# Tying a transform's input differences and conversions into program order, and loading the second stage's input one step earlier

## The chip, the cores and the metric

The kernel runs as one program on one core of a Trainium2 chip. The metric is the device time of one execution in microseconds (us), as a median over runs. Engines are written as in the profile: PE (TensorE matmul), PEld (its weight load), DVE (VectorE), ACT (ScalarE), POOL (GpSimd), SP (SyncE, which only issues DMAs here).

## The reference, cut to what matters

Three models stand one behind the other, over 8 sequences ("batches" below) of 3072 tokens with 256 channels, all in float32.

```python
X = np.fft.rfft(x, axis=1)                       # the transform, per batch and channel
y = np.fft.irfft(X * (filt_r + 1j * filt_i), n=3072, axis=1)
x_prev = shifted y, zeros in front
xk = mu_k * y + (1 - mu_k) * x_prev;  xr = mu_r * y + (1 - mu_r) * x_prev
k = np.maximum(xk @ w_k, 0);  v = (k * k) @ w_v  # 256 -> 1024 -> 256
r = 1 / (1 + np.exp(-(xr @ w_r)))
z = r * v
h = maximum of z @ w1, z @ w2, z @ w3            # 256 -> 768
out = h @ w_out                                  # 768 -> 256
```

## The kernel before, in words

**Float32 by parts.** Most matrix products take each operand as a high part and a low part (`mm3`, three matmuls for one product). `split` (L249) makes the parts of a source: ACT copies it to the high part with a cast, and POOL (or DVE) subtracts the high part from the source for the low one.

**The transform.** The first batch has its own code (`fft_first`). Batches 2 to 8 use `fft`, in three phases. In the a-phase 12 units are formed: `a_diff` (8 of 12) subtracts two halves of a loaded tile `xz` into `xd` with one DVE instruction; `a_sum` (4 of 12) adds three slices of two tiles `xr` into `xs` with four DVE instructions; `a_halves` splits the result into `xah` (ACT) and `xal` (POOL); `a_mm` multiplies it one step later (three matmuls, `pa<-xah`, `pa<-xal`, `pa<-xah`), and ACT copies the product out (`ao`) and stores it to DRAM (`s1a`, `s1b`). In the b-phase (12 steps) `b_load` loads the stored tile `xb` and splits it into `xbh` and `xbl`, `b_mm` multiplies it and applies the filter; in the c-phase `c_mm` multiplies the split result `yh`, `yl`.

**The main work.** Each batch is cut into 4 chunks, 32 in all. For a chunk `kv` runs the first feed-forward model: products `pk`, `kr` (ACT and DVE), its parts `khi` and `klo`, then `pv` three blocks later; `x2` multiplies by the gate (`gate<-pv`). For each pair of chunks `second` runs the maxima as seven products per block (`pb`, `pa`, `pe` over streamed weights `ws`, evacuated to `m`, `sc`, `u`, `v`), then `po`. Weights arrive through SP: `piece_of` asks for them 8 tiles ahead into 10 buffers (L337).

**What sets the order.** `drive` writes the transform of the next batch in small weighted pieces between the pieces of the main work. That is the program order. A scheduler of the framework then orders each engine's queue anew by a timeline that it computes, with program order as priority: an instruction whose inputs it holds to be ready may be placed ahead of work written in front of it. `tc.keep_in_program_order(ins)` takes this freedom from one instruction: it stays behind the instruction written last on its engine. Once ordered, an engine runs its queue in that order, and an instruction that waits holds all behind it. Buffers come from rotating pools (`fin`, which holds `xd`, `xs` and `xb`, has 2; `fhi`, `flo` and `filt` have 3).

Of the kernel before, what the change touches and what calls it, by code (L numbers as in the profile page):

```python
# [9 lines left out]
F32 = mybir.dt.float32  # L10
# [4 lines left out]
ALU = mybir.AluOpType  # L15
# [8 lines left out]
NK = 2 * N2  # L24
NR = 3
NS = N1 // NR * 2
GA = NG // NR
# [170 lines left out]
def tile_spectral_moe(ctx: ExitStack, tc, x, xr, xz, filt, ones, wa, wa1, wi, wbc, wb1, wc1, filt1, filt0, mu, w_k, w_v, w_r, w1, w2, w3, w_out, out):  # L198
    nc = tc.nc
    B = xr.shape[0]  # L200
    P = 128
    C = 256
# [13 lines left out]
    fp = ctx.enter_context(tc.tile_pool(name="fp", bufs=2))  # L216
# [10 lines left out]
    def mm3(o, parts, rhs_parts, onto=False, more=False):  # L227


        n = len(parts)  # L230
        for k in range(n):
            (wh, wl), (xh, xl) = parts[k], rhs_parts[k]
            mm(o, wh, xh, k == 0 and not onto, False, more)
            mm(o, wh, xl, False, False, more)
            mm(o, wl, xh, False, k == n - 1, more)
# [10 lines left out]
        nc.scalar.dma_start(mu_s, mu)  # L246
        nc.vector.tensor_scalar(nmu_s, mu_s, -1.0, 1.0, op0=ALU.mult, op1=ALU.add)

    def split(hi, lo, src, lo_eng=None):  # L249
        nc.scalar.copy(hi, src)  # L250
        (lo_eng or nc.gpsimd).tensor_tensor(lo, src, hi.bitcast(F32), ALU.subtract)  # L251


# [146 lines left out]
    def fft(b):  # L400

        s1a = dp.tile([NM, 4, GA, C], F32, tag="s1a", name=f"s1a_{b}")
        s1b = dp.tile([NM, 4, GB, C], F32, tag="s1b", name=f"s1b_{b}")
        s2 = dp.tile([NM, 4, NG, C], F32, tag="s2", name=f"s2_{b}")
        s2_of[b] = s2
        st = {}
        pieces = []
        H = NK // 2

        def x_load(t):  # L410
            st["x", t] = fp.tile([NK, NR, C], F32, tag="filt", name="xr", bufs=3)
            nc.sync.dma_start(st["x", t], xr[b, t])

        def z_load(t):
            st["z", t] = fp.tile([NK, 2, 2, C], F32, tag="filt", name="xz", bufs=3)
            nc.sync.dma_start(st["z", t], xz[b, t])

        def a_halves(u, v):
            hi = fp.tile([NK, 2, C], F32R, tag="fhi", name="xah", bufs=3)
            lo = fp.tile([NK, 2, C], F32R, tag="flo", name="xal", bufs=3)  # L420
            split(hi, lo, v, nc.gpsimd)
            st["a", u] = hi, lo

        def a_diff(u, t):
            z = st.pop(("z", t))
            v = fp.tile([NK, 2, C], F32, tag="fin", name="xd")
            nc.vector.tensor_tensor(v, z[:, 0], z[:, 1], ALU.subtract)  # L427
            a_halves(u, v)

        def a_sum(u, t):  # L430
            v = fp.tile([NK, 2, C], F32, tag="fin", name="xs")
            for k in range(2):
                x0 = st.pop(("x", t + k))
                nc.vector.tensor_tensor(v[:, k], x0[:, 0], x0[:, 1], ALU.add)
                nc.vector.tensor_tensor(v[:, k], v[:, k], x0[:, 2], ALU.add)
            a_halves(u, v)

        def a_mm(u):
            t, k = divmod(u, 3)
            w = 0 if k == 1 else 1  # L440
            hi, lo = st.pop(("a", u))
            p = ps.tile([NK, 2, C], F32, tag="pm", name="pa")
            mm3(p, [(wa_s[:, 0, w], wa_s[:, 1, w])], [(hi, lo)])
            o = fp.tile([NK, 2, C], F32, tag="fo", name="ao")
            nc.scalar.copy(o, p)
            if w == 0:
                d = s1a[8 * t : 8 * t + 8].rearrange("(k j) r g c -> (j r g) k c", k=2)
            else:
                m = 8 * t + 2 * k
                d = s1b[m : m + 4].rearrange("(k j) r g c -> (j r g) k c", k=2)  # L450
            nc.scalar.dma_start(d, o)

        NU3 = NM // 8 * 3
        NBS = NG // 2
        for u in range(NU3 + 1):
            def pa(u=u):
                t, k = divmod(u, 3)
                if u == 0:
                    z_load(0)
                if u < NU3:  # L460
                    if k == 0:
                        x_load(2 * t)
                        x_load(2 * t + 1)
                        a_diff(u, 2 * t)
                    elif k == 1:
                        z_load(2 * t + 1)
                        a_sum(u, 2 * t)
                    else:
                        if 2 * t + 2 < NM // 4:
                            z_load(2 * t + 2)  # L470
                        a_diff(u, 2 * t + 1)
                if u >= 1:
                    a_mm(u - 1)
            pieces.append((0.69, pa))

        def b_load(s):
            w = fp.tile([NK, 4, 2, NK], F32R, tag="wbc", name="wbc", bufs=3)
            nc.sync.dma_start(w.bitcast(F32), wbc_d[s].bitcast(F32))
            f = fp.tile([NK, 2, 2, C], F32, tag="filt", name="filt", bufs=3)
            nc.sync.dma_start(f, filt[:, s])  # L480
            t = fp.tile([NK, 2, C], F32, tag="fin", name="xb")
            sv, k = (s1a, 2 * s) if 2 * s < GA else (s1b, 2 * s - GA)
            nc.sync.dma_start(t, sv.rearrange("m r g c -> (m r) g c")[:, k : k + 2, :])
            hi = fp.tile([NK, 2, C], F32R, tag="fhi", name="xbh", bufs=3)
            lo = fp.tile([NK, 2, C], F32R, tag="flo", name="xbl", bufs=3)
            split(hi, lo, t)
            st["b", s] = w, f, hi, lo

        def b_mm(s):
            w, f, hi, lo = st.pop(("b", s))  # L490
            p = ps.tile([NK, 2, C], F32, tag="pm", name="pb")
            for g in range(2):
                mm3(p[:, g], [(w[:, 0, g], w[:, 1, g])], [(hi[:, g], lo[:, g])], g > 0, True)

            fr, fi = f[:, 0], f[:, 1]
            H = NK // 2
            nc.vector.scalar_tensor_tensor(fi[:H], p[H:], -1.0, fi[:H], ALU.mult, ALU.mult)
            nc.vector.tensor_tensor(fi[H:], p[:H], fi[H:], ALU.mult)
            nc.vector.tensor_tensor(fr, p, fr, ALU.mult)
            (nc.gpsimd).tensor_tensor(fr, fr, fi, ALU.add)  # L500
            yh = fp.tile([NK, 2, C], F32R, tag="fhi", name="yh", bufs=3)
            yl = fp.tile([NK, 2, C], F32R, tag="flo", name="yl", bufs=3)
            split(yh, yl, fr)
            st["c", s] = w, yh, yl

        def c_mm(s):
            w, yh, yl = st.pop(("c", s))
            p = ps.tile([NK, 2, C], F32, tag="pm", name="pc")
            for g in range(2):
                mm3(p[:, g], [(w[:, 2, g], w[:, 3, g])], [(yh[:, g], yl[:, g])], g > 0, True)  # L510
            o = fp.tile([NK, 2, C], F32, tag="fo", name="co")
            nc.scalar.copy(o, p)
            nc.scalar.dma_start(s2.rearrange("m r g c -> (m r) g c")[:, 2 * s : 2 * s + 2, :], o)

        for s in range(NBS + 2):
            def pb(s=s):
                if s < NBS:
                    b_load(s)
                if 1 <= s <= NBS:
                    b_mm(s - 1)  # L520
            def pc(s=s):
                if s >= 2:
                    c_mm(s - 2)
            pieces.append((0.65, pb))
            if s == 0:

                pieces.append((6.0, lambda: None))
            pieces.append((0.65, pc))
        return pieces
# [456 lines left out]
    s, left = second(0)  # L986
    units += s
    units.append((0.0, lambda: combos(1)))
    for p in range(1, NPAIR):
# [5 lines left out]
        s, left = second(p)  # L995
# [21 lines left out]
    for b in range(B):  # L1017
        part = units[starts[b] : ends[b]]
        if b + 1 < B:
            side = fft(b + 1)  # L1020
            cut = cuts[b] + n2 - starts[b]
            if b == 0:
                for _, fn in part[:lead]:
                    fn()
                part, cut = part[lead:], cut - lead
            drive(part[:cut], side, sum(w for w, _ in part[:cut]), sum(w for w, _ in side))
            for _, fn in part[cut:]:
                fn()
        else:
            for _, fn in part:  # L1030
                fn()
# [50 lines left out]
```

## Time and profile before

| | |
|---|---|
| median of 3 runs | 3163.63 us (3161.4 to 3163.87) |
| the profiled execution | 3161.27 us, of which the span of instructions is 3159.5 us |
| PE busy / PEld busy | 3080.0 us (97%) / 3020.4 us (96%) |
| DVE / ACT / POOL busy | 1922.4 / 1884.8 / 1858.6 us (61%, 60%, 59%) |
| granted TensorE clock, mean | 0.99 of full speed |

Busy time is summed over instructions. A wait is put down to the engine or transfer that ended last before the waiting instruction began. In timelines a bracket behind a row is the idle time of the engine just before it and what ended it. Rows of a timeline that follow each other with the same shape are merged, with their count.

### The profile page before, as it was taken

The page shows a single profiled execution, that of the slowest core. Times are in us where ns is not written, and L with a number is a line of the kernel's source. Part 1 is how long each engine was busy: PE and PEld are TensorE (multiplying, and loading weights), DVE is VectorE, ACT ScalarE, POOL GpSimd, SP SyncE. Part 2 cuts the span into 40 slices and gives each one's busy share as a digit, 9 for nine tenths or more (in the row PEclk, how much of TensorE's full clock was granted, in tenths as well). Part 3 has the DMA queues.
Part 4 walks back from the last instruction along what each step waited for, and adds up shares of the span by engine and source line. Part 5 has one row for each costly group of instructions (what it writes and reads, how often), then busy time and mean ns, then how long its engine had stood idle before and what let it go on. Part 6 is the DMA issues. An engine that isn't in the chain of part 4 may idle for free.

```text
span 3159.5 us, 55818 instructions
## 1 busy us (share of the span) xinstructions
PE 3080.0 (97%) x19172; PEld 3020.4 (96%) x19172; DVE 1922.4 (61%) x3050; ACT 1884.8 (60%) x3968; POOL 1858.6 (59%) x1591
## 2 busy tenths in 40 slices
PE   6799999999999999999999999999999999999998
PEld 4699999999999999999999999999999999999998
DVE  4976676556664666556655566656666566555554
ACT  5556656566565566656666556566666566555554
POOL 3545765567554676556756566556765468444443
PEclk8899999999999999999999999999999999999999
DMA  9878787667776677758767587765887567555554
GB/s 298 267 260 285 235 305 227 188 197 251 260 233 184 224 240 227 254 171 259 251 221 220 183 263 261 227 205 183 262 268 237 180 214 232 178 169 165 161 170 122
DMA packets 400951, 705.92 MB, mean 223 GB/s; under 512 B 41472, under 2 KB 153120, under 8 KB 400032
## 3 DMA queue, kind: packets, MB, share of 16 engines
q1 hardware_dynamic: 333648, 621.26, 62.1%
q10 hardware_dynamic: 64576, 72.45, 6.5%
q0 software_dynamic: 2448, 8.65, 0.8%
q8 instruction: 155, 2.54, 0.3%
q14 instruction: 124, 1.02, 0.1%
HBM read 616.35 MB, written 92.14 MB: 224 GB/s over the span
## 4 chain that ended last, share of the span: by engine, by line
PE 81%; DVE 6%; DMA 5%; POOL 3%; issue 3%; ACT 1%; ACTq 0%; SPq 0%; POOLq 0%; DVEq 0%
PE pb L225 17%; PE pk L225 15%; PE pv L225 14%; PE po L225 12%; PE pe L225 8%; PE pa L225 5%; PE pr L225 4%; PE py L225 3%; DMA ws<-wud 3%; PE pc L225 2%; DVE sc L773 1%; POOL klo L251 1%; DMA s<-e 1%; DVE xd L427 1%; POOL hh L251 1%
## 5 line engine op out<-in xcount | busy, mean ns | idle before, releaser
L225 PE MATMUL pb<-x,ws 128*128 128x384 f32 x3456 | 751.7, 337 | 10.2 <-DMA ws<-wud 7.0
L251 POOL TENSOR_TENSOR hh<-m,hh 128x384 fp32r<-128x384 f32 x384 | 409.5, 1075 | 563.5 <-ACT hh L250 481.4
L251 POOL TENSOR_TENSOR klo<-kr,khi 128x384 fp32r<-128x384 f32 x492 | 520.8, 1064 | 233.2 <-ACT khi L250 205.1
L225 PEld LDWEIGHTS pb<-x,ws 128*128 128x128 f32 x3456 | 596.1, 188 | 20.5 <-issue 6.4
L741 DVE SCALAR_TENSOR_TENSOR kr<-pk,kr 128x384 f32<-128x384 f32 x512 | 281.4, 553 | 429.7 <-ACT kr L740 427.5
L225 PE MATMUL pv<-khi,ws 128*128 128x384 f32 x2048 | 481.3, 338 | 4.9 <-ACT khi L250 4.9
L225 PE MATMUL po<-wo_hi,hh 128*128 128x256 f32 x2304 | 481.4, 282 | 3.3 <-ACT hh L250 2.6
L250 ACT CAST khi<-kr 128x384 fp32r<-128x384 f32 x512 | 261.9, 513 | 226.8 <-DVE kr L741 191.9
L225 PEld LDWEIGHTS po<-wo_hi,hh 128*128 128x128 f32 x2304 | 391.1, 189 | 5.0 <-ACT hh L250 3.4
L225 PE MATMUL pe<-x,ws 128*128 128x384 f32 x1728 | 387.8, 338 | 3.5 <-DVE m L848 1.4
L225 PEld LDWEIGHTS pv<-khi,ws 128*128 128x128 f32 x2048 | 358.9, 188 | 8.5 <-ACT khi L250 6.4
L225 PE MATMUL pk<-xh,wk_hi 128*128 128x384 f32 x1024 | 341.2, 336 | 3.8 <-ACT xh L250 3.8
L225 PE MATMUL pk<-xl,wk_hi 128*128 128x384 f32 x1024 | 343.7, 336 | 0.9 <-DVE xl L251 0.9
L225 PE MATMUL pk<-xh,wk_lo 128*128 128x384 f32 x1024 | 343.3, 335 | 0.0
L225 PE MATMUL po<-wo_lo,hh 128*128 128x256 f32 x1152 | 316.8, 282 | 0.0
L740 ACT ACTIVATE kr<-pk 128x384 f32<-128x384 f32 x512 | 249.8, 489 | 108.8 <-POOL klo L251 56.8
L225 PEld LDWEIGHTS pe<-x,ws 128*128 128x128 f32 x1728 | 297.4, 188 | 8.8 <-DVE sc L855 3.1
L225 PE MATMUL pv<-klo,ws 128*128 128x384 f32 x1024 | 298.6, 338 | 2.4 <-DVE klo L251 1.3
L856 DVE TENSOR_TENSOR m<-sc,m 128x384 f32<-128x384 f32 x384 | 293.9, 768 | 8.4
L251 POOL TENSOR_TENSOR xl<-xm,xh 128x768 fp32r<-128x768 f32 x126 | 234.9, 1880 | 70.3 <-ACT xh L250 70.2
L250 ACT CAST hh<-m 128x384 fp32r<-128x384 f32 x384 | 192.6, 514 | 123.5 <-DVE m L856 85.6
L809 ACT COPY v<-pb 128x384 f32<-128x384 f32 x288 | 138.3, 480 | 188.8 <-PE pb L225 181.4
(134 smaller groups left out, 6143.1 us busy)
## 6 DMA issues: line engine op xcount, KB each, us to landing
ws<-wud SPq DMA_DIRECT2D x864, 256.0 KB, 3.8
ws<-wvd SPq DMA_DIRECT2D x512, 256.0 KB, 3.7
wbc<-wbcd SPq DMA_DIRECT2D x84, 512.0 KB, 5.5
filt<-in_filt SPq DMA_DIRECT2D x84, 512.0 KB, 4.3
ws<-wud SPq DMA_DIRECT2D x288, 128.0 KB, 3.7
xz<-in_xz SPq DMA_DIRECT2D x56, 512.0 KB, 5.2
cin<-s SPq DMA_DIRECT2D x64, 384.0 KB, 4.1
out_dram<-osb ACTq DMA_DIRECT2D x192, 128.0 KB, 2.9
```

Source lines behind the costliest of these rows:

```text
L225: nc.tensor.matmul(o, lhsT=wgt, rhs=rhs, start=start, stop=stop, skip_group_check=more)
L250: nc.scalar.copy(hi, src)
L251: (lo_eng or nc.gpsimd).tensor_tensor(lo, src, hi.bitcast(F32), ALU.subtract)
L427: nc.vector.tensor_tensor(v, z[:, 0], z[:, 1], ALU.subtract)
L740: nc.scalar.activation(r, p, AF.Relu)
L741: nc.vector.scalar_tensor_tensor(r, p, 0.0, r, ALU.max, ALU.mult)
L773: eng.tensor_tensor(t, a, b, ALU.subtract)
L809: nc.scalar.copy(st[to], st[of])
L856: nc.vector.tensor_tensor(m, c, m, ALU.max)
```

## The change

The subtraction in `a_diff` and the first addition of each pair in `a_sum` (DVE) are tied into program order. The cast that makes `xbh` from the loaded `xb` (ACT) is tied too. `b_load` now only loads `xb`, and a new `b_split` one step later loads the weights and the filter and splits; `b_mm` and `c_mm` follow one step later each, in 15 steps in place of 14.

```diff
-    def split(hi, lo, src, lo_eng=None):
-        nc.scalar.copy(hi, src)
+    def split(hi, lo, src, lo_eng=None, tied=False):
+        ins = nc.scalar.copy(hi, src)
+        if tied:
+            tc.keep_in_program_order(ins)
         (lo_eng or nc.gpsimd).tensor_tensor(lo, src, hi.bitcast(F32), ALU.subtract)
...
-            nc.vector.tensor_tensor(v, z[:, 0], z[:, 1], ALU.subtract)
+            tc.keep_in_program_order(nc.vector.tensor_tensor(v, z[:, 0], z[:, 1], ALU.subtract))
             a_halves(u, v)
...
-                nc.vector.tensor_tensor(v[:, k], x0[:, 0], x0[:, 1], ALU.add)
+                tc.keep_in_program_order(nc.vector.tensor_tensor(v[:, k], x0[:, 0], x0[:, 1], ALU.add))
                 nc.vector.tensor_tensor(v[:, k], v[:, k], x0[:, 2], ALU.add)
...
         def b_load(s):
+            st["f", s] = fp.tile([NK, 2, C], F32, tag="fin", name="xb")
+            sv, k = (s1a, 2 * s) if 2 * s < GA else (s1b, 2 * s - GA)
+            nc.sync.dma_start(st["f", s], sv.rearrange("m r g c -> (m r) g c")[:, k : k + 2, :])
+
+        def b_split(s):
+            t = st.pop(("f", s))
             w = fp.tile([NK, 4, 2, NK], F32R, tag="wbc", name="wbc", bufs=3)
             nc.sync.dma_start(w.bitcast(F32), wbc_d[s].bitcast(F32))
             f = fp.tile([NK, 2, 2, C], F32, tag="filt", name="filt", bufs=3)
             nc.sync.dma_start(f, filt[:, s])
-            t = fp.tile([NK, 2, C], F32, tag="fin", name="xb")
-            sv, k = (s1a, 2 * s) if 2 * s < GA else (s1b, 2 * s - GA)
-            nc.sync.dma_start(t, sv.rearrange("m r g c -> (m r) g c")[:, k : k + 2, :])
             hi = fp.tile([NK, 2, C], F32R, tag="fhi", name="xbh", bufs=3)
             lo = fp.tile([NK, 2, C], F32R, tag="flo", name="xbl", bufs=3)
-            split(hi, lo, t)
+            split(hi, lo, t, tied=True)
             st["b", s] = w, f, hi, lo
...
-        for s in range(NBS + 2):
+        for s in range(NBS + 3):
             def pb(s=s):
                 if s < NBS:
                     b_load(s)
                 if 1 <= s <= NBS:
-                    b_mm(s - 1)
+                    b_split(s - 1)
+                if 2 <= s <= NBS + 1:
+                    b_mm(s - 2)
             def pc(s=s):
-                if s >= 2:
-                    c_mm(s - 2)
+                if s >= 3:
+                    c_mm(s - 3)
```

The queues are ordered anew as a whole. **Place 1**, DVE in the first batch's `kv`, where the transform of the second batch begins; before (`hs` belongs to the conversion of weights, `xm` to the next chunk's input):

```order
L427 TENSOR_TENSOR xd<-xz 128x512
L251 TENSOR_TENSOR klo<-kr,khi 128x384
L434 TENSOR_TENSOR xs<-xr 128x256 x2
L435 TENSOR_TENSOR xs<-xs,xr 128x256
L741 SCALAR_TENSOR_TENSOR kr<-pk,kr 128x384
L435 TENSOR_TENSOR xs<-xs,xr 128x256
L715 SCALAR_TENSOR_TENSOR xm<-yt,nmu_s,xm 128x384 x4
L741 SCALAR_TENSOR_TENSOR kr<-pk,kr 128x384
L251 TENSOR_TENSOR klo<-kr,khi 128x384
L427 TENSOR_TENSOR xd<-xz 128x512
L741 SCALAR_TENSOR_TENSOR kr<-pk,kr 128x384
```

and now, from the same first `xd` on:

```order
L429 TENSOR_TENSOR xd<-xz 128x512
L253 TENSOR_TENSOR klo<-kr,khi 128x384
L748 SCALAR_TENSOR_TENSOR kr<-pk,kr 128x384
L722 SCALAR_TENSOR_TENSOR xm<-yt,nmu_s,xm 128x384 x4
L748 SCALAR_TENSOR_TENSOR kr<-pk,kr 128x384 x2
L253 TENSOR_TENSOR klo<-kr,khi 128x384
L368 TENSOR_TENSOR hs<-ps,hs 128x4x128
```

The four additions and the second difference have left this place; they now stand some 40 instructions of the main work later, in `second` of the first pair.

**Place 2**, PE in a later batch (the fourth that `fft` serves), at the fourth unit of the a-phase; before (`pa_` and `pb_` with numbers are products of `second`; `pa<-xah` and `pa<-xal` are the transform's):

```order
L225 MATMUL pb_15294<-x_15037,ws 128x384 x3
L225 MATMUL pe_15390<-x_15040,ws 128x384 x3
L225 MATMUL pa<-xah,wa_s 128x512
L225 MATMUL pa<-xal,wa_s 128x512
L225 MATMUL pa<-xah,wa_s 128x512
L225 MATMUL pb_15382<-x_15029,ws 128x384 x3
L225 MATMUL pa_15383<-x_15032,ws 128x384 x3
```

and now, the same unit:

```order
L225 MATMUL pv<-klo,ws 128x384 x2
L225 MATMUL pb_15294<-x_15043,ws 128x384 x3
L225 MATMUL pe_15346<-x_15046,ws 128x384 x3
L225 MATMUL pb_15338<-x_15037,ws 128x384 x3
L225 MATMUL pe_15390<-x_15040,ws 128x384 x3
L225 MATMUL pb_15382<-x_15029,ws 128x384 x3
L225 MATMUL pa_15383<-x_15032,ws 128x384 x3
L225 MATMUL pb_15338<-x_15043,ws 128x384 x3
L225 MATMUL pa<-xah,wa_s 128x512
L225 MATMUL pb_15448<-x_15022,ws 128x384 x3
```

The unit stands at about the same point of the main work, and its three matmuls no longer stand together: the one on the low part comes nine matmuls behind the first.

**Place 3**, DVE for the same unit; before:

```order
L856 TENSOR_TENSOR m<-sc,m 128x384
L852 TENSOR_TENSOR m<-pb_14410,m 128x384
L855 TENSOR_TENSOR sc<-pe_14489,v 128x384
L427 TENSOR_TENSOR xd<-xz 128x512
L856 TENSOR_TENSOR m<-sc,m 128x384
```

and now:

```order
L855 TENSOR_TENSOR m<-pe_15346,v 128x384
L859 TENSOR_TENSOR m<-pa_15339,m 128x384
L769 TENSOR_TENSOR gate<-pv,gate 128x384 x2
L429 TENSOR_TENSOR xd<-xz 128x512
L855 TENSOR_TENSOR m<-pe_15346,u 128x384
L862 TENSOR_TENSOR sc<-pe_15390,v 128x384
L863 TENSOR_TENSOR m<-sc,m 128x384
```

The difference stood in the blocks of the pair before (products 14410 and 14489); now it stands behind the gate product of the chunk that has just ended, among blocks 15339 to 15390.

## Rows read from the trace of the kernel before

**Rows 1.** The page, part 1: busy us, share, instructions.
```profile
PE 3080.0 (97%) x19172; PEld 3020.4 (96%) x19172; DVE 1922.4 (61%) x3050; ACT 1884.8 (60%) x3968; POOL 1858.6 (59%) x1591
```
**Rows 2.** Busy us by engine in stretches of the span, columns in the first row.
```profile
core 0: us, PE busy (x) PEld busy (x) DVE busy (x) ACT busy (x) POOL busy (x), PEclk, DMA share, GB/s
160.00:200.00 40.00, 35.88 (x236) 34.34 (x235) 37.92 (x51) 22.63 (x47) 27.88 (x24) 0.99 0.76 248
240.00:300.00 60.00, 59.35 (x368) 57.56 (x369) 46.94 (x67) 40.10 (x85) 40.28 (x33) 1.00 0.88 295
480.00:2743.00 2263.00, 2251.41 (x14174) 2225.34 (x14174) 1381.68 (x2197) 1387.50 (x2937) 1402.75 (x1191) 1.00 0.70 225
2743.00:3050.00 307.00, 307.00 (x1916) 307.00 (x1916) 160.15 (x272) 176.15 (x382) 145.45 (x133) 1.00 0.54 163
```
**Rows 3.** Waits of PE from 480 to 2743 us: total us, times, longest.
```profile
PE pb L225 <- DMA ws<-wud: 6.5, 11, 1.2
PE pa L225 <- DMA ws<-wud: 1.7, 3, 0.7
```
**Rows 4.** Timeline of DVE at place 1: start, us, instruction.
```profile
185.19 3.69 DVE L434 TENSOR_TENSOR xs<-xr 128x256 f32<-128x256 f32 x2
188.81 0.41 DVE L435 TENSOR_TENSOR xs<-xs,xr 128x256 f32<-128x256 f32 x1
...
189.94 3.99 DVE L715 SCALAR_TENSOR_TENSOR xm<-yt,nmu_s,xm 128x384 f32<-128x384 f32 x4
193.86 0.55 DVE L741 SCALAR_TENSOR_TENSOR kr<-pk,kr 128x384 f32<-128x384 f32 x1
...
195.94 2.31 DVE L427 TENSOR_TENSOR xd<-xz 128x512 f32<-128x512 f32 x1
198.17 0.54 DVE L741 SCALAR_TENSOR_TENSOR kr<-pk,kr 128x384 f32<-128x384 f32 x1
```
**Rows 5.** Timeline of PE and ACT at the same place.
```profile
195.26 0.62 PE L225 MATMUL pv<-khi,ws 128*128 128x384 f32 x2 [1.34 <-ACT khi L250]
...
198.75 0.51 ACT L250 CAST khi<-kr 128x384 fp32r<-128x384 f32 x1 [1.78 <-DVE kr L741]
...
199.32 0.56 PE L225 MATMUL pv<-khi,ws 128*128 128x384 f32 x1 [1.83 <-ACT khi L250]
```
**Rows 6.** Busy us from 180 to 240 us, `xd` alone, then `xs` alone (DVE, ACT, POOL).
```profile
180.00:240.00 60.00, 4.72 (x4) 1.86 (x3) 4.20 (x3) 0.97 0.80 273
...
180.00:240.00 60.00, 5.87 (x8) 0.64 (x1) 1.29 (x1) 0.97 0.80 273
```
**Rows 7.** Instructions of the a-phase over the run: count, ns min/median/max, first and last start.
```profile
L427 DVE TENSOR_TENSOR xd<-xz x56: 675/1406/2308, 182.9 to 2434.9; 128x512 f32<-128x512 f32 x56
...
L250 ACT CAST xah<-xd x56: 610/623/634, 191.2 to 2445.4; 128x512 fp32r<-128x512 f32 x56
L251 POOL TENSOR_TENSOR xal<-xd,xah x56: 1263/1298/1746, 191.9 to 2446.2; 128x512 fp32r<-128x512 f32 x56
```
**Rows 8.** Timeline at places 2 and 3, ACT, DVE, then PE.
```profile
1256.17 0.62 ACT L250 CAST xah<-xd 128x512 fp32r<-128x512 f32 x1
...
1271.28 1.02 DVE L762 TENSOR_TENSOR gate<-pv,gate 128x384 f32<-128x384 f32 x2 [0.68 <-PE pv L225]
...
1274.38 0.39 PE L225 MATMUL pa<-xah,wa_s 128*128 128x512 f32 x1
...
1283.95 1.72 PE L225 MATMUL pb<-x,ws 128*128 128x384 f32 x9
```
**Rows 9.** A wait of PE near place 2, and SP's waits from 1250 to 1280 us.
```profile
1277.08 1.12 PE L225 MATMUL pb<-x,ws 128*128 128x384 f32 x5 [0.79 <-DMA ws<-wud]
...
SPq L416 <- DVE xd L427: 3.6, 1, 3.6
```
**Rows 10.** A DMA (KB, median us to landing), and ACT's waits for `xb` over the run.
```profile
xz<-in_xz SPq DMA_DIRECT2D x56, 512.0 KB, 5.2
...
ACT xbh L250 <- DMA xb<-s1a: 15.0, 12, 2.2
```

## The prediction, made before the changed kernel ran

> **What bounds the kernel now.** I read the page's busy times first. PE is busy for 97% of the span, and no other engine for more than 61% [rows 1]. So the time is PE's work plus the moments in which PE stands still, and an edit that takes no matmul away can only move those moments. The second view, busy time by stretches, says where they are [rows 2]. From 160 to 200 us PE idles for 40 - 35.88 = 4.1 us, and DVE is busy for 37.92 of these 40. From 240 to 300 us PE idles for 0.65 us. From 480 to 2743 us, in which six of the seven changed transforms run, PE idles for 2263 - 2251.41 = 11.6 us in all. From 2743 to 3050 us no transform runs, and PE doesn't idle at all. The reader is to see how little there is to win. The third view, PE's waits from 480 to 2743 us, says what the 11.6 us are: 8.2 us (6.5 + 1.7 us, 14 waits) are for streamed weights `ws` [rows 3], which the change doesn't touch directly.
>
> [...]
>
> **Part 1: the early differences leave the first batch (place 1).** On DVE the four additions of `a_sum` took 3.69 us (two of them, merged) and 0.41 us for a third, with another like it, some 4.5 us. They stood in front of `xm` and of the `kr` at 193.86 us [rows 4]. PE then waited 1.34 us for `khi`, which is made from that `kr`, and again 1.83 us at 199.32 us, where `khi` had waited 1.78 us for the `kr` at 198.17 us; just ahead of this one DVE had run `xd` for 2.31 us [rows 4, 5]. The order shows both groups gone from here. DVE could then start the first `kr` up to 4.5 us and the second up to 2.3 us sooner, more than either wait. I take both waits as gone: -3.2 us. Bounds: -4.1 us (all idle time of the stretch) and 0, if `kr` is late by its own product.
>
> **Part 2: they reappear in a shorter stretch of the first batch.** From 180 to 240 us `xd` and `xs` took 4.72 + 5.87 = 10.6 us of DVE [rows 6]. All but the first `xd` (about 1 us) move behind 240 us. The stretch from 240 to 300 us had 46.94 us of DVE work [rows 2]; with 9.6 us more it is 56.5 of 60, or 94%. What PE loses beside a DVE that full isn't shown there, so I bound it by the two nearest rows. At 78% it lost 0.65 us in 60 us. At 95% (160 to 200 us) it lost 4.1 us in 40, which is 6.2 us in 60. The cost lies between 0 and 5.5 us; I take the middle, +2.8 us, since the order still has matmuls of `second` to fill with there, while the earlier stretch had products that hung on DVE directly.
>
> **Part 3: in the six later batches the a-phase loses its lead.** Before, the cast of the fourth unit's `xah` ended at 1256.79 us and its product began at 1274.38 us, 17.6 us later [rows 8]. Now the tied difference stands behind the two `gate` products, which wait for the last `pv<-klo` (place 3), and PE reaches the unit after 21 matmuls from there (place 2). One takes between 307.00 / 1916 = 0.16 us, an average with narrower ones among them [rows 2], and 1.72 / 9 = 0.19 us, which counts the drain of the last [rows 8]; I take 0.17 us, so 21 take 3.6 us. The chain against it is `gate` twice, 1.02 us [rows 8], `xd` 1.41 us and `xah` 0.62 us [rows 7], and three handovers of about 0.05 us (DVE's `kr` ends at 198.71 us, ACT's `khi` begins at 198.75 us [rows 4, 5]): 3.2 us. The unit comes 0.4 us early. Its low part takes POOL 1.30 us more [rows 7], 4.5 us, and is wanted nine matmuls later, at 5.2 us: early by 0.7 us. So a lead of 17 us becomes one of half a microsecond, at one of the tightest of 12 units. With `xd` at its longest, 2.31 us [rows 7], the unit is 0.5 us late. In a batch 8 of 12 units go through `xd`. If all 8 were 0.5 us late, six batches would lose 24 us; if none, nothing. I take one such delay for each batch, 0.5 us, hence +3 us, nearer to nothing: main chains with as many links through DVE, ACT and POOL cost PE next to nothing from 480 to 2743 us, where waits for `ws` alone make 8.2 of 11.6 us [rows 2, 3].
>
> The tie adds a wait for `xz` as well. It lands 5.2 us after issue [rows 10], and behind a held `xd` stand the `m` and `sc` of the blocks (place 3). I cost it at nothing: a buffer of `filt` is free two pieces of the transform ahead, and DVE has work for only 61% of the time. If that cover is gone, each microsecond that `xz` is late holds the evacuation of `second`.
>
> **Part 4: SP is freed of a block.** Near place 2 SP waited 3.6 us to load an `xz` into a buffer that a late `xd` still held, with `ws` loads queued behind, and PE waited 0.79 us for `ws` soon after [rows 9]. Now the differences run at their own place, and the loads stand closer together. It may take these waits away or make them longer: -8.2 to +8.2 us. Of 8.2 us of `ws` waits I take a good third as gone, -3 us, the share that I put down to starts of a transform.
>
> **Part 5: the b-phase.** ACT stood 15.0 us over the run for `xb` that had not landed, 12 times [rows 10]. The load one step ahead ends that. I cost both this and the later casts at nothing. ACT is busy for 60% of the time, and none of PE's waits in the later batches is for these products [rows 3]. The `wbc` and `filt` loads keep their distance of one step to the product. Bounds: 15 us of ACT time would be a gain only if PE hung on it; a loss as in part 3 would be 12 units by half a microsecond in a batch, but here the order leaves more matmuls between cast and product.
>
> **Sum.** -3.2 + 2.8 + 3.0 - 3.0 + 0 = -0.4 us on the profiled execution's 3161.3 us: 3160.9 us. The median of the runs lies 2.4 us above that execution, so I forecast 3163 us, no change (0.2% is 6.3 us, about what a measurement of this kernel can tell from none).
>
> **Rivals.**
>
> *Faster.* Part 1 comes in full, part 4 ends all waits for `ws` in the later batches, and nothing new is late: -3.2 - 8.2 = -11.4 us, 3152 us. For it: the block of SP and the two waits are plain rows [rows 5, 9]. Against it: 14 small waits at different places seldom have one cause.
>
> *Slower: the tied differences come late for their products.* The place is the a-phase of every batch, the price 0.5 us for each unit that is late, and it decides from about a dozen late units over the seven transforms more than I took. With half of the 8 units late in six batches (12 us), the crowded stretch at its upper bound (5.5 us), part 1 as taken (-3.2) and nothing from part 4: +14.3 us, 3178 us. For it: the lead is spent, and the matmuls of a unit are now torn apart, which shows that its parts become ready one by one. Against it: the worked unit is still early at median durations.
>
> [...]
>
> That the change doesn't do what it says is no rival: the order shows the differences moved.
>
> **How the numbers follow.** Forecast (within 0.2%, 3157 to 3169 us): 38%. Faster rival and what lies between: 33%. Slower by late differences: 24%, by the lock: 5%. So faster 0.33, same 0.38, slower 0.29. The range runs from 3149 us (the faster rival with its bound of part 1, and some 2 us of other waits) to 3178 us (the slower one); I leave out some 8% below and 10% above. The forecast's own range is 3157 to 3169 us.
>
> **What would show it.** Part 1: no waits of over a microsecond for `khi` between 190 and 200 us. Part 2: DVE above 90% from 240 to 300 us, and PE idle 2 to 4 us there. Part 3: waits of `pa` for `xah` or `xal` in PE's list, some half a microsecond per batch; more than 9 us in all would make the forecast wrong on the slow side. Part 4: the waits of `pb` and `pa` for `ws` at about 5 us in place of 8.2; under 2 us would make it wrong on the fast side. Part 5: no wait of ACT for `xb`, and none of PE for `xbh`.

## The result: 0.6% slower

The changed kernel takes 3181.72 us (median of 6 runs, 3178.69 to 3185.99), the kernel before 3162.89 us beside it (6 runs, 3160.21 to 3163.87): a ratio of 1.0062, 95% interval [1.0049, 1.0075]. The forecast was 3163 us and its range ended at 3178 us, so the change is slower than forecast, and outside the range. The profiled execution of after took 3181.95 us, with a span of 3180.2 us, 20.7 us longer than before.

The page of after, part 1, in the columns of [rows 1]:

```profile
PE 3086.6 (97%) x19172; PEld 3025.1 (95%) x19172; DVE 1932.4 (61%) x3050; ACT 1888.1 (59%) x3968; POOL 1852.0 (58%) x1591
```

The instructions are as many as before on every engine. PE's busy time is 6.6 us longer for the same 19172 matmuls. For PE, busy time is not a sum over instructions: matmuls of 128x384 take 0.33 us and start 0.17 us apart (rows in the last section), and overlapping ones count once. The last matmul before a gap then counts in full, which may be what adds the 6.6 us; no run shows it by itself. The stretches of after, in the columns of [rows 2]:

```profile
160.00:200.00 40.00, 37.59 (x251) 36.45 (x250) 35.85 (x48) 23.95 (x50) 30.16 (x26) 1.00 0.74 241
240.00:300.00 60.00, 56.61 (x348) 53.87 (x348) 47.25 (x72) 39.61 (x83) 39.95 (x32) 1.00 0.88 296
480.00:2743.00 2263.00, 2237.98 (x14044) 2209.46 (x14044) 1391.34 (x2191) 1379.89 (x2917) 1387.74 (x1183) 1.00 0.71 225
2743.00:3050.00 307.00, 307.00 (x1932) 307.00 (x1931) 160.57 (x270) 176.74 (x382) 153.16 (x140) 1.00 0.53 161
```

PE idles 25.0 us from 480 to 2743 us where it idled 11.6 [rows 2], and 130 fewer matmuls fit in. The first batch changes little: 4.1 us become 2.4 from 160 to 200 us, 0.65 become 3.4 from 240 to 300. The loss is in the later batches, and PE's waits there (us in total, times, longest), against [rows 3], name it:

```profile
PE pa L225 <- ACT xah L250: 12.5, 15, 2.3
PE pb L225 <- DMA ws<-wud: 4.2, 9, 0.9
PE pv L225 <- POOL klo L253: 3.9, 12, 0.5
PE pv L225 <- ACT khi L250: 2.7, 2, 2.4
```

The waits for `ws` fell from 8.2 to 4.2 us. New are 12.5 us for `xah`. Most of it is one hole per batch. The timelines show it near 509, 890, 1270, 1651, 2031 and 2413 us, with idle times of 2.38, 2.30, 1.49, 2.30, 2.28 and 1.49 us (the first for `khi`, the others for `xah`), 12.2 us in six batches. The hole at 1270 us, in the timelines of PE, ACT, DVE and POOL of after (start, us, instruction):

```profile
1264.47 0.50 PE L225 MATMUL pa<-xah,wa_s 128*128 128x512 f32 x1 [0.26 <-ACT xah L250]
...
1270.07 0.50 PE L225 MATMUL pa<-xah,wa_s 128*128 128x512 f32 x1 [1.49 <-ACT xah L250]
...
1269.40 0.62 ACT L250 CAST xah<-xs 128x512 fp32r<-128x512 f32 x1 [0.37 <-DVE xs L437]
...
1262.25 1.51 DVE L429 TENSOR_TENSOR xd<-xz 128x512 f32<-128x512 f32 x1
1263.69 1.23 DVE L436 TENSOR_TENSOR xs<-xr 128x256 f32<-128x256 f32 x1
1264.84 1.64 DVE L780 TENSOR_TENSOR sc<-sc,gate 128x384 f32<-128x384 f32 x1
1266.40 0.55 DVE L780 TENSOR_TENSOR sc<-gate 128x384 f32<-128x384 f32 x1
1266.88 0.41 DVE L437 TENSOR_TENSOR xs<-xs,xr 128x256 f32<-128x256 f32 x1
1267.21 0.41 DVE L436 TENSOR_TENSOR xs<-xr 128x256 f32<-128x256 f32 x1
1267.55 0.55 DVE L780 TENSOR_TENSOR sc<-gate,sc 128x384 f32<-128x384 f32 x1
1268.01 1.02 DVE L253 TENSOR_TENSOR x<-sc,x 128x384 fp32r<-128x384 f32 x2
1268.95 0.41 DVE L437 TENSOR_TENSOR xs<-xs,xr 128x256 f32<-128x256 f32 x1
...
1263.18 1.45 POOL L253 TENSOR_TENSOR x<-sc,x 128x384 fp32r<-128x384 f32 x1
1264.59 1.48 POOL L253 TENSOR_TENSOR xal<-xd,xah 128x512 fp32r<-128x512 f32 x1
```

Read it from the bottom of DVE's rows up. The unit is the second of the batch, an `a_sum`. Its last addition stands at 1268.95 us, behind `sc` and `x` of the next pair. These are the work of `combos`, which is written in front of the whole transform; the scheduler has spread them among the additions. The tie shows in the middle: the first addition of the second pair (1267.21 us) is tied behind the second addition of the first pair (1266.88 us), written just before it, and so can't move up. `xah` follows the last addition, and PE has nothing left in front of the product. The DVE rows from 1262.25 to 1266.48 us are also slow: 1.51, 1.23 and 1.64 us for forms that take 0.68, 0.41 and 0.55 us elsewhere, and the last two end 0.3 and 0.4 us after the POOL instruction beside them.

Slow rows lengthen the hole. At 890 us DVE's order is the same, but the last addition took 1.21 us beside a POOL instruction in place of 0.41, and the hole is 2.30 us in place of 1.49. The same holds at 1651 and 2031 us, with 1.21 us beside a POOL instruction of 1.17 us and holes of 2.30 and 2.28 us. At 1270 and 2413 us it took 0.41 us, though it too stands beside a POOL instruction, one of 1.51 us.

```profile
889.91 0.50 PE L225 MATMUL pa<-xah,wa_s 128*128 128x512 f32 x1 [2.30 <-ACT xah L250]
...
887.99 1.21 DVE L437 TENSOR_TENSOR xs<-xs,xr 128x256 f32<-128x256 f32 x1
...
887.75 1.17 POOL L253 TENSOR_TENSOR x<-sc,x 128x384 fp32r<-128x384 f32 x1 [2.65 <-ACT x L250]
```

### The profile page after: what moved, and what is told of

It is laid out like the page before. It is cut to its first block, busy times and chain, and to the rows that moved or that the text cites. A ratio compares the mean times of both kernels' runs of the same rounds, so it can differ in the third digit from the quotient of the medians.

```text
span 3180.2 us, 55593 instructions
## 1 busy us (share of the span) xinstructions
PE 3086.6 (97%) x19172; PEld 3025.1 (95%) x19172; DVE 1932.4 (61%) x3050; ACT 1888.1 (59%) x3968; POOL 1852.0 (58%) x1591
## 4 chain that ended last, share of the span: by engine, by line
PE 81%; DVE 7%; POOL 5%; DMA 3%; issue 3%; ACT 1%; ACTq 0%; POOLq 0%; SPq 0%; DVEq 0%
PE pb L225 19%; PE pk L225 13%; PE po L225 13%; PE pv L225 13%; PE pe L225 9%; PE pa L225 6%; PE pr L225 4%; PE py L225 3%; PE pc L225 2%; POOL klo L253 2%; DMA ws<-wud 1%; POOL x L253 1%; DVE sc L780 1%; POOL yl L253 1%; DMA ws<-wvd 1%
## 5 line engine op out<-in xcount | busy, mean ns | idle before, releaser
L253 POOL TENSOR_TENSOR hh<-m,hh 128x384 fp32r<-128x384 f32 x384 | 402.4, 1056 | 569.5 <-ACT hh L250 459.9
L225 PE MATMUL pv<-khi,ws 128*128 128x384 f32 x2048 | 468.7, 337 | 8.5 <-ACT khi L250 8.5
L863 DVE TENSOR_TENSOR m<-sc,m 128x384 f32<-128x384 f32 x384 | 334.5, 875 | 9.7
L225 PE MATMUL pv<-klo,ws 128*128 128x384 f32 x1024 | 287.8, 340 | 7.0 <-POOL klo L253 4.1
```

Source lines behind the costliest of these rows:

```text
L225: nc.tensor.matmul(o, lhsT=wgt, rhs=rhs, start=start, stop=stop, skip_group_check=more)
L863: nc.vector.tensor_tensor(m, c, m, ALU.max)
```

## The experiments

All ratios are to the kernel before, on the same chip, with 95% intervals. None of the 18 kernels is faster than it. They are called e1 to e18.

**One part of the change at a time.** First (e1) the kernel before with the ties of the differences alone.

```diff
-            nc.vector.tensor_tensor(v, z[:, 0], z[:, 1], ALU.subtract)
+            tc.keep_in_program_order(nc.vector.tensor_tensor(v, z[:, 0], z[:, 1], ALU.subtract))
...
-                nc.vector.tensor_tensor(v[:, k], x0[:, 0], x0[:, 1], ALU.add)
+                tc.keep_in_program_order(nc.vector.tensor_tensor(v[:, k], x0[:, 0], x0[:, 1], ALU.add))
```

> The kernel before with the DVE ties alone: the difference in a_diff and the first addition of each pair in a_sum tied, b_load as it was. Theory A (the ties spend the a-phase's lead, and PE waits for xah): 15 to 22 us above before, PE's waits for xah at 9 to 14 us from 480 to 2743 us. Rival B (the split b_load with its tied cast on ACT costs the time): within 3 us of before, waits for xah under 2 us. Rival C (any new order of the queues moves the time by this much): no relation to the parts, some 5 to 15 us above before here and in the next two as well.

e1 took 3167.84 us, 1.0020 [1.0011, 1.0029]: some 6 us, not 15 to 22. PE's waits from 480 to 2743 us:

```profile
PE pa L225 <- ACT xah L250: 7.2, 11, 1.3
PE pb L225 <- DMA ws<-wud: 2.1, 2, 1.1
```

So the ties bring waits for `xah` and take some for `ws` away. By themselves they are not the whole 18.8 us.

Then (e2) the kernel after without those ties; the first addition in `a_sum` is freed likewise.

```diff
-            tc.keep_in_program_order(nc.vector.tensor_tensor(v, z[:, 0], z[:, 1], ALU.subtract))
+            nc.vector.tensor_tensor(v, z[:, 0], z[:, 1], ALU.subtract)
...
```

> The kernel after with the DVE ties taken out: only the load of xb one step earlier and its tied cast. Theory A: within 3 us of before, waits of PE for xah under 1 us. Rival B: 10 to 20 us above before. Rival C: 5 to 15 us above before.

e2 took 3202.29 us, 1.0127 [1.0113, 1.0141], slower than the change as a whole and than any of the three expected. Its longest entries are 11.5 us for `ws` and 6.3 us of PE's own issue; there is none for `xah`. The parts don't add up: about 6 and 40 us apart, 19 together.

Then (e4) the load ahead without any tie, which is e2 with

```diff
-            split(hi, lo, t, tied=True)
+            split(hi, lo, t)
```

> The kernel before with the load of xb one step ahead alone, nothing tied. Theory A: within 3 us of before; ACT's waits for xb fall from 15 us to under 2, and PE gains nothing by it. Rival B (the later steps of the b-phase, not the tie, cost the time): 8 to 15 us above before. Rival C: 5 to 15 us above before.

e4 took 3181.55 us, 1.0061 [1.0049, 1.0074]. Moving a load by a step, which the prediction cost at nothing, takes 20 us alone, more than any of the three expected. PE's longest waits from 480 to 2743 us are all for tiles of the main work:

```profile
PE pb L225 <- ACT v L816: 5.1, 5, 1.2
PE pb L225 <- DMA ws<-wud: 3.9, 4, 1.2
PE pc L225 <- DVE m L859: 2.5, 5, 0.5
```

**The product moved back.** If the lead of the a-phase is what is lost, a second step between difference and product should give it back (e3, the kernel after with one edit).

```diff
-        for u in range(NU3 + 1):
+        for u in range(NU3 + 2):
...
-                if u >= 1:
-                    a_mm(u - 1)
+                if u >= 2:
+                    a_mm(u - 2)
```

> The kernel after, with the a-phase's product written two steps behind the difference in place of one (a_mm(u - 2), one step more in the loop). Theory A: the lead grows by one step of some 6 us, PE's waits for xah from 480 to 2743 us fall from 12.5 us to under 2, and the time by 9 to 13 us against the kernel after, to 3169 to 3173 us. Rival B: unchanged within 3 us, 3179 to 3185 us. A second rival to A's cure, that DVE held by the tied differences costs PE through the main work and not through xah: waits for xah vanish, and the time falls by less than 4 us.

e3 took 3176.94 us, 1.0045 [1.0031, 1.0058]. The waits for `xah` fell from 12.5 to 5.6 us, and waits for `khi` rose from 2.7 to 11.4 us. None of the three had that. The hole at the second unit stayed, 1.1 us in each of five batches, and that makes the 5.6 us. The new waits for `khi` stand elsewhere, near 1072, 1453, 1834, 2215 and 2598 us with 1.7 us each; what makes them is not shown.

**Only the places moved.** The change makes the list of weighted pieces longer by one step, so `drive` writes the whole transform at other points of the main work. Three kernels test that by the weights of the pieces of the b- and c-phase alone: e5 is the kernel after and e6 is e4, both with 14/15, which puts the steps back to nearly their old places; e7 is the kernel before with 15/14.

```diff
-            pieces.append((0.65, pb))
+            pieces.append((0.65 * 14 / 15, pb))
...
-            pieces.append((0.65, pc))
+            pieces.append((0.65 * 14 / 15, pc))
```

> The kernel after with the weights of the b- and c-pieces scaled by 14/15, so that the longer list of pieces weighs what it did before and each unit of the a-phase is written at the old point of the main work. Theory P (the longer list moves all units of the transform against the main work, and that costs): about the ties alone, 3165 to 3171 us, with the wait of the a-phase's second unit at 0.6 us a batch in place of 1.5 to 2.3. Theory L (the load apart from its conversion costs by itself): 3179 to 3185 us, as the kernel after.

> The load of xb one step ahead, nothing tied, with the same scaled weights. Theory P: within 3 us of before. Theory L: 15 to 23 us above before, as with the weights unscaled.

> The kernel before with the weights of the b- and c-pieces scaled by 15/14, nothing else: the list weighs what the longer one does, and the units of the transform move against the main work as in the kernel after. Theory P: 8 to 20 us above before. Theory L: within 3 us of before. If every new order costs, whatever makes it: above before as well, by some 5 to 20 us.

e5 took 3184.46 us, 1.0065 [1.0052, 1.0079], against 3165 to 3171 expected. e6 took 3171.21 us, 1.0026 [1.0017, 1.0035], so at the old places the load ahead costs some 8 us in place of 20. e7 took 3191.82 us, 1.0090 [1.0076, 1.0104]: the kernel before, with no instruction and no tie changed, loses more than under the whole change. Its waits from 480 to 2743 us:

```profile
PE pe L225 <- DVE gate L762: 12.3, 5, 3.3
PE pv L225 <- ACT khi L250: 10.4, 6, 1.7
```

The counterpart is e12, the kernel before with 14/15; e13 and e14 are two small moves of it, by 1.01 and 0.99:

```diff
-            pieces.append((0.65, pb))
+            pieces.append((0.65 * 1.01, pb))
...
-            pieces.append((0.65, pc))
+            pieces.append((0.65 * 1.01, pc))
```

> The kernel before with the pieces of the b- and c-phase weighted 14/15 in place of 1 and no other edit: the counterpart of the run with 15/14, which cost 29 us. Theory M (any move of the points at which the transform is written costs, since the order before is one that was found by trying): 8 to 30 us slower, 3170 to 3192 us, in waits of PE spread over khi, klo, m and gate. Rival D (it was the direction of the move, the transform written later, that cost): 3158 to 3167 us.

> The kernel before with the pieces of the b- and c-phase weighted 1.01 in place of 1 and no other edit: the transform is written at slightly other points and the queues come out in another order, with the same work. Theory M (the order before is a settled one, and an order that is not settled costs 5 to 30 us whatever makes it): 3168 to 3192 us. Rival E (the kernel after loses by what its edits do; a small move costs nothing): 3157 to 3167 us.

> The kernel before with the pieces of the b- and c-phase weighted 0.99 and no other edit. Theory M: 3168 to 3192 us. Rival E: 3157 to 3167 us.

e12 took 3185.82 us, 1.0075 [1.0063, 1.0088]; e13 3167.69 us, 1.0023 [1.0014, 1.0032]; e14 3166.86 us, 1.0015 [1.0006, 1.0024]. Moves of 7% either way cost 24 and 29 us, moves of 1% about 5. The small moves fall where the two theories meet, e13 between their ranges and e14 just inside the rival's: they cost something, and less than theory M had it. The kernel before stands at the lowest of the five points tried.

The same small moves of the kernel after, in the same two lines, are e15 (1.01) and e16 (0.99):

> The kernel after with the pieces of the b- and c-phase weighted 1.01 and no other edit. Theory M: the kernel after is one of many orders, so its neighbours scatter about it by as much as those of before scatter, 3168 to 3195 us, and may be faster than it by more than 5 us. Rival E: within 5 us of the kernel after, 3177 to 3187 us, with the waits of PE for xah of the second unit (12 us from 480 to 2743 us) still there.

> The kernel after with the pieces of the b- and c-phase weighted 0.99 and no other edit. Theory M: 3168 to 3195 us, and not the same waits as in the kernel after. Rival E: 3177 to 3187 us, with the waits of PE for xah of the second unit still there.

e15 took 3188.04 us, 1.0082 [1.0069, 1.0096], and e16 3189.07 us, 1.0087 [1.0073, 1.0101]. They are slower by 6 and 7 us than after. Their waits for `xah` and `khi` from 480 to 2743 us, e15, then e16:

```profile
PE pa L225 <- ACT xah L250: 14.1, 15, 2.3
PE pv L225 <- ACT khi L250: 4.2, 7, 2.4
```

```profile
PE pv L225 <- ACT khi L250: 14.2, 11, 2.4
...
PE pa L225 <- ACT xah L250: 2.8, 3, 2.3
```

Both times lie in theory M's range and above rival E's, though e15 keeps the waits for `xah` that rival E named. From e15 to e16 the names changed places and the size stayed. That is the clue.

**Where and when: the first transform, and the cast.** e8 is e1 with both ties only in the second batch.

```diff
+            if b == 1:
+                tc.keep_in_program_order(ins)
```

> The kernel before with the DVE ties in the first of the seven transforms alone. With the ties in all transforms PE was 4.5 us ahead of before at 499 us and lost 1.3 us in each later batch. If gain and loss belong to their places: 4 to 5 us below before, 3156 to 3158 us, and the later batches as before, with no wait for xah. If the order of the whole run hangs together: anything within 10 us of before.

e8 took 3166.91 us, 1.0015 [1.0006, 1.0024]. The gain that was expected from clearing the first batch did not come. PE idles 11.7 us from 480 to 2743 us, as in the kernel before, and 1.7 us less from 160 to 200 us, but 3.8 us more from 240 to 480 us.

e9 is the kernel after and e10 is e5, both with the cast free; e11 is the kernel before with the opposite edit.

```diff
-            split(hi, lo, t, tied=True)
+            split(hi, lo, t)
```

> The kernel after, with the cast of xbh left free; the differences stay tied and the load stays one step ahead. Theory C (the tied cast holds ACT's queue, as the load ahead with the tied cast took 20.7 us more than the load ahead alone): 8 to 15 us under the kernel after, 3167 to 3174 us, with the waits of PE for xah still there (10 to 15 us from 480 to 2743 us), since those come of the tied additions at the moved places. Rival R (each edit only leads to another order, and none has a price of its own): within 5 us of the kernel after, 3177 to 3187 us, with other waits in place of those that go.

> The kernel after with the pieces of the b- and c-phase weighted 14/15, so that the transform is written at nearly its old points of the main work, and with the cast of xbh left free. Theory C: only the ties of the differences (+6 us measured alone) and the load ahead at the old points (+8 us) are left, 3166 to 3176 us, without waits of PE for xah over 1 us. Rival R: no lower than with the tied cast at the old points, 3180 to 3188 us.

> The kernel before with the cast of xbh tied into program order and nothing else: the load of xb stays in the same step, right ahead of the cast. [...] Rival R: the tie alone costs little, 3160 to 3170 us.

e9 took 3180.08 us, 1.0063 [1.0049, 1.0077]; e10 3172.11 us, 1.0035 [1.0023, 1.0048]; e11 3181.73 us, 1.0061 [1.0048, 1.0074]. In the kernel after the tied cast bears under 2 us, at the old places 12, alone in the kernel before 20. Theory C's time came true in e10 and failed in e9, and e11 lies above rival R's 3160 to 3170 us. But that the tied cast holds ACT's queue, as theory C has it, is not shown in e11: ACT's list there has no wait for `xb` at all, where before has 15.0 us, and PE's longest waits from 480 to 2743 us are for `ws` (10.9 us), `sc` (6.6) and `klo` (4.3). From issue to landing `xb` takes 3.0 us at the least in before, and 4.6 in the median.

In e9 the hole stands at the same unit under the name of `khi`. PE and DVE of it, in the rows that answer to the hole of after:

```profile
1267.26 1.33 PE L225 MATMUL pv<-khi,ws 128*128 128x384 f32 x4 [2.37 <-ACT khi L250]
...
1263.71 1.01 DVE L253 TENSOR_TENSOR x<-sc,x 128x384 fp32r<-128x384 f32 x2
1264.64 1.21 DVE L437 TENSOR_TENSOR xs<-xs,xr 128x256 f32<-128x256 f32 x1
1265.78 0.41 DVE L436 TENSOR_TENSOR xs<-xr 128x256 f32<-128x256 f32 x1
1266.12 0.54 DVE L748 SCALAR_TENSOR_TENSOR kr<-pk,kr 128x384 f32<-128x384 f32 x1
1266.58 0.41 DVE L437 TENSOR_TENSOR xs<-xs,xr 128x256 f32<-128x256 f32 x1
```

The same additions stand behind the same `sc` and `x`; only now a `kr` waits behind them, and with it the `khi` that PE wants first. From 1240 to 1290 us PE's timeline has this hole in all eight kernels in which the differences of the later batches are tied: 1.49 us in after, 1.28 (e1), 1.11 (e3) and 2.25 (e15) for `xah`; 1.34 (e5), 2.37 (e9), 1.35 (e10) and 2.38 (e16) for `khi`. In the kernels whose additions are untied there no wait for either exceeds 0.31 us.

**The test of it: the additions left free, the subtraction tied.** e17 is the kernel after and e18 is e9, both with this edit.

```diff
-                tc.keep_in_program_order(nc.vector.tensor_tensor(v[:, k], x0[:, 0], x0[:, 1], ALU.add))
+                nc.vector.tensor_tensor(v[:, k], x0[:, 0], x0[:, 1], ALU.add)
```

> The kernel after with the additions of a_sum left free; the subtraction of a_diff and the cast stay tied. Theory H (wherever the differences are tied, PE has one hole of 1.3 to 2.5 us per batch at the second unit, an a_sum, whose additions stand among the sc and x of the next pair, and it is named xah in one kernel and khi in another): the hole at 1255 to 1285 us goes, no wait of over 1 us for xah or khi there, 8 to 15 us under the kernel after, 3167 to 3174 us. Rival M (only the order as a whole decides): anywhere from 3168 to 3195 us, with the hole or others as large still there.

> The kernel after with the additions of a_sum and the cast of xbh left free; only a_diff stays tied, and the load stays one step ahead. Theory H: no hole at the second unit; 8 to 15 us under the kernel after with the cast free (3180 us), 3165 to 3172 us. Rival M: 3168 to 3195 us, with the hole or others as large still there.

e17 took 3169.42 us, 1.0023 [1.0013, 1.0033], and e18 3166.12 us, 1.0014 [1.0005, 1.0023]. Both are as theory H expected: 12.3 us under after, and 14.0 under e9. (Each against the kernel before beside it, the falls are 11.1 and 14.4 us.) Waits of e17 from 480 to 2743 us, and PE and DVE at the second unit:

```profile
PE pb L225 <- DMA ws<-wud: 6.8, 8, 1.5
PE pv L225 <- POOL klo L253: 6.2, 17, 0.5
PE pa L225 <- ACT xah L250: 2.2, 10, 0.2
```

```profile
1265.40 0.50 PE L225 MATMUL pa<-xah,wa_s 128*128 128x512 f32 x1 [0.19 <-ACT xah L250]
...
1260.31 2.65 DVE L436 TENSOR_TENSOR xs<-xr 128x256 f32<-128x256 f32 x2
1262.89 0.55 DVE L780 TENSOR_TENSOR sc<-sc,gate 128x384 f32<-128x384 f32 x1
1263.36 0.54 DVE L780 TENSOR_TENSOR sc<-gate 128x384 f32<-128x384 f32 x1
1263.83 0.75 DVE L437 TENSOR_TENSOR xs<-xs,xr 128x256 f32<-128x256 f32 x2
```

Free, both first additions stand ahead of `sc`, the two second ones follow together behind two `sc`, and the third `sc` and the two `x` come behind the last addition and no longer in front of it. In after these three hold it for 1.4 us (1267.55 to 1268.95 us), and the wait here is 1.3 us shorter, 0.19 in place of 1.49. The hole has not gone to nothing everywhere: in e18 five batches have a wait of 1.1 us for a `kr` behind `x<-sc,x`, less than half of what it replaces.

From 480 to 2743 us of e17 PE's idle time falls by less than the holes, from 25.0 to 17.9 us, because the waits for `ws` and `klo` grow:

```profile
480.00:2743.00 2263.00, 2245.12 (x14117) 2217.00 (x14117) 1376.70 (x2201) 1388.48 (x2928) 1398.37 (x1188) 1.00 0.71 226
```

## Why the prediction was wrong

The step that failed is part 3. It worked the lead out on one unit, an `xd`, priced the lateness at 0.5 us per batch on the 8 units that go through `xd`, and never worked the 4 that go through `xs`. The worked unit itself did come early, by 0.9 us where the sum had 0.4 (its cast ends at 1284.28 us, its product begins at 1285.17 us). But the cast of an `a_sum` needs the last of four additions, and the tie holds two of them back among `sc` and `x`. One of the four such units in a batch, the second of all twelve, comes late by more than 0.3 us. That the delay is one for each batch was right, by luck, since it was worked out on another unit; its price was not. The measured term is about 2 us in each batch, 12.2 us in six, where +3.0 stood. Waits for `xah` above 9 us were named as the sign that would make the forecast wrong on the slow side, and 12.5 us came. With the additions free some 11 to 12 us of the 18.8 go.

Part 1: PE idles 1.7 us less from 160 to 200 us, not 3.2. The direction was right, and the ties of that transform alone gained nothing in the end (e8). Part 2: PE lost 2.7 us more from 240 to 300 us, close to the +2.8 taken, but not for the reason given. DVE is busy for 47.25 of 60 us, 79%, and not for 94%. PE's waits there are those of part 3, for the two parts of a unit:

```profile
PE pa L225 <- POOL xal L253: 1.8, 1, 1.8
PE pa L225 <- ACT xah L250: 1.0, 1, 1.0
```

Part 4: the `ws` waits fell by 4.0 us where 3.0 stood; this was right in size, but SP was not freed. From 1250 to 1280 us it still waits 3.0 us in one piece to load an `xz`, for an addition now, where it waited 3.6 us for `xd` [rows 9]. So the size is luck as far as the runs show. Part 5: ACT's waits for `xb` left its list, and one wait of PE for `xbh` came, 1.2 us in the first batch. Yet a cost of nothing for the later load and casts was wrong: the load ahead alone cost 20 us and the tied cast alone 20 us, through waits of the main work elsewhere. In the kernel after, the cast bears 1.6 us (against e9), and with the additions free 3.3 us (e17 against e18). On top of the tied differences the load ahead adds 12 us (e1 to e9); the holes grow from 1.3 to 2.4 us with it.

Behind part 5 stands something the prediction left out. It took the order apart at two or three places, while the change orders the queues anew everywhere. Weights alone cost the kernel before 5 to 29 us with the same work, so an edit cannot be priced by its own instructions only.

Of the rivals, the slower one by late differences had the right mechanism and, by luck, nearly the time (3178 us): its 12 us were 24 units late by 0.5 us, not 6 late by 2. It named the wrong units. The 5% for a lock of DVE and POOL was the author's guess, and no run shows such a lock. What the runs show is slow DVE rows: at the hole three DVE instructions took 4.38 us together where 1.64 us are their short times, with POOL busy beside them; yet the last addition there took its 0.41 us with POOL busy beside it too. The slowness isn't enough by itself: in e17, with the additions free, two of them take 2.65 us where their short times make 0.82, and PE waits 0.19 us. But in the tied order it adds 0.8 us to three of the six holes, and at 1270 us the three slow rows lost 2.74 us, more than the hole of 1.49. No run shows what makes the rows slow, and none took the slowness away with the order kept, so how much of the 12.2 us is its share stays open.

What stays open: why the load ahead without ties (e4) and with the tied cast (e2) lose 20 and 40 us, when tying the subtraction as well brings them to 3166 us (e18) and 3169 us (e17). The waits of e2 and e4 are spread over `ws`, `v`, `m` and `filt`, and no run took one of them away by itself. Nor has a tie one price. The ties of the differences cost 6 us on the kernel before (e1), but only 1 to 3 us on e6 (e10, with its holes of 1.35 us) and nothing on e4 (e9, 1.5 us faster), and they gain 20 us on e2 (the kernel after): beside the hole that they make, they move other waits. Nor is it shown which of the remaining 4 us of e18 are the edit's and which the order's.

## What to carry to other kernels

Before tying an instruction to its written place, follow every unit that goes through it, the longest chain first: here one unit in each batch, of the 4 in 12 that have two tied additions, made most of PE's new idle time, while the 8 with one tied subtraction can stay tied at 3166 to 3169 us. Where a scheduler orders the queues, measure first what a change with no work in it (a weight moved by 1% or 7%) does to the time; that is the noise an edit has to beat, and here none of 18 other orders was faster than the kernel before. When a wait goes and the time stays, look at what stands in the same engine's queue at the same place: the wait may only have changed its name.

## Not expected of the hardware

PE's granted clock fell behind some of the holes. In e9, after 2.37 us without work, the matmuls of 128x384 behind the hole took 0.53 us and came 0.32 us apart, against 0.33 and 0.17 us before it:

```profile
1262.87 0.33 PE L225 MATMUL pk<-xl,wk_hi 128*128 128x384 f32 x1
1263.05 0.33 PE L225 MATMUL pk<-xh,wk_lo 128*128 128x384 f32 x1
...
1269.12 0.53 PE L225 MATMUL pk<-xl,wk_hi 128*128 128x384 f32 x1
1269.44 0.53 PE L225 MATMUL pk<-xh,wk_lo 128*128 128x384 f32 x1
```

The granted clock was 0.94 of full speed over 1255 to 1285 us there, and 0.89 from 1270 to 1285 us in e15 behind its 2.25 us; it was 1.00 behind the 2.38 us of e16. The hole then costs more than its idle time, but not each time. An estimate from the rows of e9: the eleven matmuls from 1267.26 to 1270.72 us took 3.5 us, and at the spacing of before the hole (0.17 us, 0.23 for the wide one) they take 2.0, so the slower matmuls added some 1.5 us.
